# Inverse sequence products in five blocks of 128 frequencies instead of six, with a shifted sine table

## The chip, the cores and the metric

The kernel runs on one core of a Trainium2 chip. The time is device microseconds of one execution, as the median of several runs. The profile shows one further execution in detail: TensorE (PE, with its weight loads as PEld), VectorE (DVE), ScalarE (ACT), GpSimd (POOL), SyncE's DMA queue (SP), and the DMA engines.

## The reference

A spectral layer and a gated feed-forward layer, both on one sequence of S = 2048 rows and D = 576 columns, in bf16:

```python
x = A_x                                         # (1, 2048, 576)
X = rfft2(layernorm(x))                         # 2048 x 289 complex
y = irfft2(X * (w_r + 1j * w_i), s=(2048, 576)) # to bf16
h = x + y
n = layernorm(h)
out = h + (gelu(n @ w_gate) * (n @ w_up)) @ w_down   # 576 -> 4608 -> 576, tanh gelu
```

## The kernel before

Both transforms are matrix products. Row s of the sequence is written as 16·p + h, with p on the 128 partitions and h = 0..15 in the free dimension, so that the transform over 2048 rows splits into one over 16 and one over 128. The column transform over 576 uses only J = 289 frequencies (JP = 290 with one column of padding, JH = 145 of each parity).

The spectral layer has these stages on TensorE.

- `row16` (L259, L268): normalised rows times the table of the 16-point transform, with some filler products (L247). ScalarE copies the results to `Bt`.
- A loop over nine sequence frequencies in the order k = 1, 2, ..., 7, 0 (`order`; k = 0 also carries k = 8). One round of the loop takes care of three different groups at once: `f2` (L442) is the column transform of the newest group, `f3` (L457, L458) the 128-point transform of the group before, and `i3` (L541, L542) the first inverse product of the group three rounds back. ScalarE copies each result from PSUM to SBUF (`pq`, `g`, `hs`, `EO`).
- Between `f3` and `i3`, VectorE forms sums (`sums_of`, L487 and L488), multiplies with the complex weights `WR`, `WI` (L505), combines the four products (L511, L512), and writes the result to one of three buffers `Zt` (L516, L517). The group k = 0 is done in two halves of the columns, 0 to 127 and 128 to 288, and L511 and L512 write `Zt` directly.
- `inv_cols` (L568): the inverse column product, for half `x` of the groups and a pair `g` of rows h. ScalarE evicts the result.
- `add_rows` (L680): the inverse 16-point product. VectorE adds it to `h_sb`.

`Zt` holds four rows of JP = 290 columns: cosine and sine parts b = 0, 1, and the same with the roles exchanged (a = 1). The inverse product `i3` has the columns as output partitions. It takes them in NJT = 3 tiles of 128, the last with 33 columns and zeros behind them (each buffer has 96 columns of zeros at its end), for both b: 3 x 2 blocks, each of two matmuls (a = 0, 1) of 256 columns. So a group has 12 matmuls, and `EO` has six blocks:

```python
EO = [eop.tile([P, 2, NJT, H, 2, 4, 8], ...) for x in range(2)]
lhsT=EO[x][:, e, jt, 2 * g : 2 * g + 2], rhs=DT[:, jt, :, e, :] if jt < 2 else DI[:, :, e, :]
```

`DT` holds the cosine (e = 0) and sine (e = 1) tables of the columns 0 to 255, `DI` those of the last 33, `D3` is what `DI` is copied from in `late_tables` (L396). ScalarE computes `DT` and `D3` at L310 and L311. `TF` and `TI` are the twiddle tables; `TI` is the transposition of `TF` by a DMA on SP in `twiddles` (L382), followed on that queue by the load of `wd_a`.

The head of the feed-forward layer comes next. `add_sum` adds the inverse result to rows h = 0 to 3, and the sums for the second layernorm come with it (VectorE for the sum, ScalarE for the squares). `head_rstd` makes the mean and `rstd2` from them: two small operations on VectorE (L734, L737) and two on GpSimd (L738, and the power at L739). `norm2` and `flip` normalise rows 0 and 1 and transpose them by DMA (L717); `norm_row` and `turn` do it for rows 2 and 3 with transpositions on TensorE (L747), whose result is copied to `hl[0]` in two parts, by ScalarE (L750) and VectorE (L751). Products of `inv_cols` stand between these steps and keep TensorE busy. PSUM is used through a rotation of four double banks with the tag `two`.

Then come four blocks of 512 rows of the feed-forward layer: 36 gate/up products each (L815), with gelu on ScalarE (L823) and the product on VectorE (L824), and the down products (L835). The remaining rows are normalised beside the first of these.

The order on every engine is the order of the program text (a manual schedule); waits follow from the data.

Of the kernel before, what the change touches and what calls it, by code (L numbers as in the profile page):

```python
# [20 lines left out]
P = 128  # L21
# [9 lines left out]
NR = D // 64  # L31
NDT = 5
NJT = 3
FQ = 3
PI = 3.1415925
G_SCALE = 2.0 ** -10
# [4 lines left out]
def kernel_body(  # L41
# [65 lines left out]
    DT = keep.tile([P, 2, 2, 2, JH], BF16, name="DT")  # L107
    DF = keep.tile([P, 2, 2, JH], BF16, name="DF")
    DI = keep.tile([P, 2, 2, JH], BF16, name="DI")
    mv = keep.tile([P, H, 2], FP32, name="mv")  # L110
    rstd = keep.tile([P, H], FP32, name="rstd")
    mv2 = keep.tile([P, H, 2], FP32, name="mv2")
# [50 lines left out]

    TF = sp.tile([P, 9, 3, P], BF16, name="TF")
    TI = sp.tile([P, 9, 3, P], BF16, name="TI")
    Zts = [sp.tile([P, 4 * JP + 96], BF16, name=f"Zt{i}") for i in range(3)]

    scr_pool = tc.tile_pool(name="scr", bufs=1, side="right")
    scr = scr_pool.__enter__()
# [160 lines left out]
    V.tensor_scalar(F16[:, 2, :], F16[:, 0, :], -1.0, None, op0=ALU.mult)  # L330
    ln_rstd(rstd, mv, 0, 4)
    for z in Zts:
        G.memset(z[:, 4 * JP :], 0.0)
        G.memset(z[:, J : 4 * JP : JP], 0.0)
    sd(4, 6)
    fin(5, 7)
    norms(0, 4)
# [40 lines left out]


    def twiddles():  # L380
        A.activation(TF[:, :, 1, :], ab[:], ACT.Sin, bias=nhpib[:], scale=2.0 * PI / S)
        nc.sync.dma_start(  # L382
            TI[:].rearrange("p k r q -> p (k r) q"), TF[:].rearrange("p k r q -> p (k r q)"), transpose=True
        )
        nc.sync.dma_start(wd_a[:], wd_view[:, 0:NWA, :])

    def weights():

# [4 lines left out]
            V.tensor_scalar(w[:, :, 0 : J : J - 1], w[:, :, 0 : J : J - 1], 0.5, None, op0=ALU.mult)  # L393

    def late_tables():
        V.tensor_copy(DI[0 : J - 2 * P], D3[0 : J - 2 * P])  # L396
        pt = two("pt")
        for x in range(2):
            for p0 in (0, 64):
                T.matmul(  # L400
                    pt[p0 : p0 + 64, 0, x * P : (x + 1) * P],
                    lhsT=F16[:, 0, 64 * x : 64 * x + 64],
                    rhs=ident[:],
                    start=True,
                    stop=True,
                )
# [83 lines left out]
    def wmul(k, i, nxt=None):  # L490
        x = xab[k]
        z = Zts[i % 3]
        zt[k] = z
        zv = z[:, 0 : 4 * JP].rearrange("p (a b j) -> p a b j", a=2, b=2)
        sl = slice(k, 18 - k, 17 - 2 * k) if k else slice(0, 9, 8)
        m1, m2 = (wk.tile([P, 2, 2, JP], BF16, name=n, tag=n, bufs=1) for n in ("m1", "m2"))
        if k:
            za, zb = (wk.tile([P, 2, JP], BF16, name=n, tag=n, bufs=1) for n in ("za", "zb"))
        else:
            za, zb = zv[:, 0], zv[:, 1]  # L500

        for j0, j1 in ((0, J),) if k else ((0, P), (P, J)):
            js = slice(j0, j1)
            for w, m in ((WR, m1), (WI, m2)):
                V.tensor_tensor(  # L505
                    m[:, :, :, js],
                    x[:, :, :, js],
                    w[:, sl, js].unsqueeze(1).to_broadcast([P, 2, 2, j1 - j0]),
                    ALU.mult,
                )  # L510
            V.tensor_tensor(za[:, :, js], m1[:, 0, :, js], m2[:, 1, :, js], ALU.subtract)  # L511
            V.tensor_tensor(zb[:, :, js], m1[:, 1, :, js], m2[:, 0, :, js], ALU.add)  # L512
            if nxt:
                sums_of(nxt)
            if k:
                V.tensor_tensor(zv[:, 0, :, js], za[:, :, js], zb[:, ::-1, js], ALU.add)  # L516
                V.tensor_tensor(zv[:, 1, :, js], zb[:, ::-1, js], za[:, :, js], ALU.subtract)  # L517

    eo = {}

    def i3(k, jt):


        z = zt[k]
        x, i = place[k]

        def zl(a, b):
            o = (2 * a + b) * JP + jt * P
            return z[:, o : o + P]

        n = 2 if k and jt < 2 else 1
        if jt == 0 or n == 1:
            eo[k] = two("eo_ps")
        if k:
            ps = eo[k][:].rearrange("p b (n h e l) -> p b n e h l", n=2, h=H, l=8)[:, :, jt % n]
            parts = ((0, k, (0, 0), (1, 1)), (1, k, (0, 1), (1, 0)))
        else:
            ps = eo[k][:, 0, :].rearrange("p (e h b l) -> p b e h l", e=2, h=H, l=8)
            parts = ((0, 0, (0, 0), (1, 0)), (1, 8, (0, 1), (1, 1)))
        for b, kk_, z0, z1 in parts:  # L540
            T.matmul(ps[:, b], lhsT=zl(*z0), rhs=TI[:, kk_, 1:3, :], start=True, stop=False)  # L541
            T.matmul(ps[:, b], lhsT=zl(*z1), rhs=TI[:, kk_, 0:2, :], start=False, stop=True)  # L542
        if n == 2:
            if jt == 1:
                A.copy(
                    EO[x][:, :, 0:2, :, :, i, :].rearrange("p b t h e l -> p b (t h e) l"),
                    eo[k][:].rearrange("p b (r l) -> p b r l", l=8),
                )
        elif k:
            A.copy(  # L550
                EO[x][:, :, jt, :, :, i, :].rearrange("p b h e l -> p b (h e) l"),
                eo[k][:, :, 0 : 2 * P].rearrange("p b (r l) -> p b r l", l=8),
            )
        else:
            (V.tensor_copy if jt == 1 else A.copy)(
                EO[x][:, :, jt, :, :, i, :].rearrange("p e h b l -> p e (h b) l"),
                eo[k][:, 0, :].rearrange("p (e r l) -> p e r l", e=2, l=8),
            )

    cs = {}  # L560
# [2 lines left out]
    def inv_cols(x, g):  # L563

        ps = two("cs_ps")
        for e in range(2):
            for jt in range(NJT):
                T.matmul(  # L568
                    ps[:, e, 0:JP],
                    lhsT=EO[x][:, e, jt, 2 * g : 2 * g + 2].rearrange("p h e k l -> p (h e k l)"),  # L570
                    rhs=DT[:, jt, :, e, :] if jt < 2 else DI[:, :, e, :],
                    start=(jt == 0),
                    stop=(jt == NJT - 1),
                )
# [22 lines left out]
    for i in range(n + 1):  # L597
# [26 lines left out]
        if i == 1:  # L624
            late_tables()
            scr_pool.__exit__(None, None, None)
            eop = ctx.enter_context(tc.tile_pool(name="eop", bufs=1, side="right"))
            EO = [eop.tile([P, 2, NJT, H, 2, 4, 8], BF16, name=f"EO{x}", tag=f"EO{x}") for x in range(2)]
    for g in range(3):
        inv_cols(0, g)  # L630
    for k in order[6:]:
# [99 lines left out]
    def head_rstd(h):  # L731


        V.scalar_tensor_tensor(  # L734
            mv2[:, h, 1:2], sums[:, h, 0:1], sums[:, h, 0:1], sums[:, h, 1:2], op0=ALU.mult, op1=ALU.subtract
        )
        V.tensor_scalar(mv2[:, h, 0:1], sums[:, h, 0:1], 1.0 / D, None, op0=ALU.mult)  # L737
        G.tensor_scalar(rstd2[:, h : h + 1], mv2[:, h, 1:2], -1.0 / (D * D), 1e-5, op0=ALU.mult, op1=ALU.add)  # L738
        G.tensor_tensor(rstd2[:, h : h + 1], rstd2[:, h : h + 1], mhalf[:, h : h + 1], ALU.pow)  # L739

    def turn(h):


        pt = psum.tile([P, 2048], BF16, name="pt", tag="two", bufs=4)
        for r in range(NR):
            for p0 in (0, 64):
                T.transpose(pt[p0 : p0 + 64, r * P : (r + 1) * P], ln2[h][:, r * 64 : (r + 1) * 64], ident[:])  # L747
        q = h % 4 * P
        pv = pt[:, 0 : NR * P].rearrange("p (r q) -> p r q", r=NR)
# [32 lines left out]
    turn(2)  # L782
    turn(3)
    inv_cols(1, 6)
    inv_cols(1, 7)
    load_wd(2)

# [113 lines left out]
```

## Time and profile before

| | |
|---|---|
| median of 3 runs | 509.99 us (509.99 to 509.99) |
| profiled execution | 509.67 us, its span 507.4 us |
| granted clock of TensorE in it | 1.0 |
| PE busy | 496.0 us (98%) |
| DVE, ACT, POOL busy | 213.9, 154.5, 33.1 us |
| L815 (gate/up) on the chain that ended last | 55% |
| L835 (down) on it | 28% |
| first gate/up matmul | 78.74 us after the start of the span |

The chain that ended last lies on TensorE for 94% of the span. All that the change edits lies ahead of the first gate/up matmul, that is, in the first 79 of 507 us. In the lines of a timeline the columns are: start, duration, engine, line, operation, output and inputs, shape, count; the idle time ahead of it and what ended that idle time stand in brackets. A matmul's duration includes its passage through the array; what one costs in a dense stream is the distance between two starts (its pitch).

### The profile page before, as it was taken

How to read it: one execution, taken by the hardware profiler on the slowest of the kernel's cores; microseconds unless marked ns; L12 is line 12 of the kernel's file. 1: busy time of each engine (PE TensorE's matmuls, PEld its weight loads, DVE VectorE, ACT ScalarE, POOL GpSimd, SP SyncE). 2: the span in 40 equal slices, each digit the busy share in tenths (PEclk: the TensorE clock that was granted, in tenths of full speed). 3: DMA queues.
4: the chain of work that ended last, by engine and by line, in shares of the span. 5: the costliest groups of instructions: out<-in, count | busy, mean ns of one | idle time of the engine just before them, and what ended most of it. 6: DMA issues, size and time to landing. Idle time of an engine off the chain costs nothing.

```text
span 507.4 us, 9925 instructions
## 1 busy us (share of the span) xinstructions
PE 496.0 (98%) x4357; PEld 288.9 (57%) x4357; DVE 213.9 (42%) x414; ACT 154.5 (30%) x266; POOL 33.1 (7%) x88
## 2 busy tenths in 40 slices
PE   6989999999999999999999999999999999999997
PEld 2557775444447774444467744444577544444775
DVE  8979963689661015433311034433201233333001
ACT  8688985322230002323310023233200132323000
POOL 8700020111110000000000000000000000000000
PEclk9999999999999999999999999999999999999999
DMA  8964057779970019997720089987500578770000
GB/s 290 237 139 141 1 165 206 148 149 195 191 143 1 0 43 199 180 201 151 149 63 0 1 186 198 182 166 152 101 1 0 119 163 158 157 152 2 13 12 25
DMA packets 86090, 60.66 MB, mean 120 GB/s; under 512 B 21920, under 2 KB 84768, under 8 KB 86048
## 3 DMA queue, kind: packets, MB, share of 16 engines
q1 hardware_dynamic: 85760, 58.85, 57.3%
q0 software_dynamic: 288, 1.18, 0.8%
q8 instruction: 34, 0.56, 0.5%
q14 instruction: 8, 0.07, 0.1%
HBM read 52.65 MB, written 2.36 MB: 108 GB/s over the span
## 4 chain that ended last, share of the span: by engine, by line
PE 94%; DVE 3%; ACT 1%; issue 0%; POOL 0%; POOLq 0%; ACTq 0%; DVEq 0%
PE gu L815 55%; PE acc L835 28%; PE cs_ps L568 2%; PE f2t L259 1%; PE pq_ps L442 1%; PE y_ps L680 1%; PE eo_ps L542 1%; PE eo_ps L541 1%; PE f2t L247 1%; PE gh_ps L457 1%; PE gh_ps L458 1%; PE f L268 1%; DVE st L119 0%; DVE st L118 0%; DVE m L505 0%
## 5 line engine op out<-in xcount | busy, mean ns | idle before, releaser
L815 PE MATMUL gu<-Bt,wgu 64*128 64x512 bf16 x2592 | 281.4, 376 | 0.0
L815 PEld LDWEIGHTS <-wgu 64*128 64x128 bf16 x2592 | 126.1, 94 | 152.2 <-issue 1.0
L823 ACT ACTIVATE g_sb<-gu 128x512 f32<-128x512 f32 x144 | 86.0, 597 | 301.9 <-PE gu L815 301.8
L824 DVE TENSOR_TENSOR P_sb<-g_sb,gu 128x512 bf16<-128x512 f32 x144 | 98.7, 685 | 151.7 <-ACT g_sb L823 151.7
L835 PEld LDWEIGHTS <-P_sb 128*128 128x128 bf16 x1152 | 112.4, 98 | 30.6 <-issue 2.4
L835 PE MATMUL acc<-wd,P_sb 128*128 128x288 bf16 x768 | 99.3, 286 | 0.0
L847 DVE TENSOR_TENSOR h_sb<-h_sb,acc 128x576 bf16<-128x576 bf16 x15 | 11.3, 754 | 118.2 <-PE acc L835 118.2
L835 PE MATMUL acc<-wd_a,P_sb 128*128 128x288 bf16 x384 | 52.3, 286 | 0.5 <-DVE h_sb L843 0.5
L247 PE MATMUL f2t<-h_sb,ident 128*128 128x512 bf16 x41 | 13.6, 459 | 4.4 <-DMA h_sb<-in_A_x_dram 4.4
L442 PE MATMUL pq_ps<-DT,Bt 128*128 128x290 bf16 x64 | 12.4, 286 | 0.0
L705 DVE TENSOR_SCALAR hrow<-h_sb,mv,rstd 128x1152 bf16<-128x1152 bf16 x14 | 12.1, 867 | 0.5 <-POOL rstd L739 0.5
L568 PE MATMUL cs_ps<-DT,EO 128*128 128x290 bf16 x64 | 12.2, 286 | 0.0
L247 PEld LDWEIGHTS <-ident 128*128 128x128 bf16 x45 | 5.0, 111 | 12.3 <-issue 6.6
L541 PE MATMUL eo_ps<-TI,Zt 128*128 128x256 bf16 x48 | 11.5, 272 | 0.4 <-DVE Zt L516 0.4
L542 PE MATMUL eo_ps<-TI,Zt 128*128 128x256 bf16 x48 | 11.5, 273 | 0.1
L136 POOL TENSOR_TENSOR rstd<-rstd,mhalf 128x1 f32<-128x1 f32 (+2 forms) x17 | 11.4, 673 | 1.4
L135 POOL TENSOR_SCALAR rstd<-mv 128x1 f32<-128x1 f32 (+2 forms) x17 | 4.0, 238 | 108.9 <-DVE mv L120 108.7
L568 PEld LDWEIGHTS <-EO 128*128 128x128 bf16 x96 | 9.0, 96 | 3.0 <-issue 0.2
L442 PEld LDWEIGHTS <-Bt 128*128 128x128 bf16 x96 | 9.2, 97 | 2.5
L450 ACT CAST pq<-pq_ps 128x580 bf16<-128x580 f32 x15 | 9.9, 660 | 0.9 <-PE pq_ps L442 0.8
L259 PE MATMUL f2t<-F,xn 128*128 128x256 bf16 x64 | 9.7, 273 | 0.3 <-DVE xn L139 0.3
L118 DVE BATCH_NORM_STATS2 st<-h_sb 128x6 f32<-128x288 bf16 x22 | 9.8, 445 | 0.0
(132 smaller groups left out, 261.0 us busy)
## 6 DMA issues: line engine op xcount, KB each, us to landing
wgu<-in_B_w_gate_dram SPq DMA_DIRECT2D x48, 432.0 KB, 5.1
wgu<-in_B_w_up_dram SPq DMA_DIRECT2D x48, 432.0 KB, 6.6
wd<-in_B_w_down_dram SPq DMA_DIRECT2D x2, 1728.0 KB, 8.0
h_sb<-in_A_x_dram SPq DMA_DIRECT2D x3, 576.0 KB, 5.9
wd_a<-in_B_w_down_dram SPq DMA_DIRECT2D x1, 1728.0 KB, 9.4
out_dram<-h_sb SPq DMA_DIRECT2D x3, 576.0 KB, 3.3
WR<-in_A_w_r_dram SPq DMA_DIRECT2D x1, 650.2 KB, 8.7
WI<-in_A_w_i_dram SPq DMA_DIRECT2D x1, 650.2 KB, 11.0
```

The costliest lines, as they stand in the source:

```text
L136: G.tensor_tensor(dst[:, sl], dst[:, sl], mhalf[:, sl], ALU.pow)
L247: T.matmul(dst, lhsT=ident[:], rhs=h_sb[:, 2, 0:512], start=True, stop=True)
L259: T.matmul(f2t[:, h % 2, t * 2 * P : (t + 1) * 2 * P], lhsT=x[:, d0 : d0 + P], rhs=F16[:, n : n + 2, :], start=(n == 0), stop=(n == 1),)
L442: T.matmul(ps[:, par, 0:JP], lhsT=Bt[:, t, col], rhs=DT[:, t // 2, par] if t < 4 else DF[:, par], start=(t == par), stop=(t == 4),)
L541: T.matmul(ps[:, b], lhsT=zl(*z0), rhs=TI[:, kk_, 1:3, :], start=True, stop=False)
L542: T.matmul(ps[:, b], lhsT=zl(*z1), rhs=TI[:, kk_, 0:2, :], start=False, stop=True)
L568: T.matmul(ps[:, e, 0:JP], lhsT=EO[x][:, e, jt, 2 * g : 2 * g + 2].rearrange("p h e k l -> p (h e k l)"), rhs=DT[:, jt, :, e, :] if jt < 2 ...
L705: V.tensor_scalar(hrow[:], h_sb[:, h, :].rearrange("p (r k) -> p r k", k=64).unsqueeze(2).to_broadcast([P, NR, 2, 64]), mv2[:, h, 0:1], rs ...
L815: T.matmul(gu[:, c, :], lhsT=w[rows, r, i * P : (i + 1) * P], rhs=hl[tcnk % 2][rows, r, :], start=(r == 0), stop=(r == NR - 1),)
L823: A.activation(g_sb[:], gu[:, 0, :], ACT.Gelu_apprx_tanh)
L824: V.tensor_tensor(p_sb(fa + i), g_sb[:], gu[:, 1, :], ALU.mult)
L835: T.matmul(acc[:, c, 0:DH], lhsT=p_sb(f)[:, st * P : (st + 1) * P], rhs=wd[f // NWA][:, f % NWA, cc], start=(f == 0), stop=(f == NFT - 1),)
```

## The change

`Zt` becomes four rows of ZS = 320 columns, 289 used and 31 zeros. For k = 1 to 7 the rows of the two parts b lie one behind the other, 640 columns, and the inverse product takes them in five tiles of 128: tiles 0 and 1 are columns 0 to 255 of b = 0, tile 2 holds columns 256 to 319 of b = 0 and 0 to 63 of b = 1, tiles 3 and 4 are columns 64 to 319 of b = 1. That makes ten matmuls of 256 columns per group. L517's operands change so that the parts lie in the order that this needs.

For the sine part, the column product now needs a table that begins at column 64. This is the new `DS`; it and the second half of the sine part of `DI` are filled by five copies by DMA on the SP queue, ahead of the transposition of the twiddles. `DI`'s copy on VectorE takes only the cosine part.

For k = 0 (and 8) the two parts come from different twiddles. There the five tiles are formed from 24 matmuls of 128 columns in place of 12 of 256; the last eight have 64 output partitions each, four for the lower and four for the upper half.

ScalarE's `EO` copies per group k = 1 to 7 are one of four blocks and one of one block (before: four and two).

In the head, the scaling for `rstd2` moves from GpSimd to VectorE, `head_rstd(3)` moves ahead of `norm2(1)`, `turn` uses one PSUM tile with one VectorE copy for row 2 and two tiles with a ScalarE and a VectorE copy for row 3, and `inv_cols(1, 6)` moves ahead of both `turn` calls. The memsets of `Zt` on GpSimd become three instead of six.

The order of TensorE's other products, of VectorE's frequency loop and of all of the feed-forward layer stays.

```diff
+ZS = 320
+    DS = keep.tile([P, 2, 2, JH], BF16, name="DS")
-    Zts = [sp.tile([P, 4 * JP + 96], BF16, name=f"Zt{i}") for i in range(3)]
+    Zts = [sp.tile([P, 4, ZS], BF16, name=f"Zt{i}") for i in range(3)]
...
     for z in Zts:
-        G.memset(z[:, 4 * JP :], 0.0)
-        G.memset(z[:, J : 4 * JP : JP], 0.0)
+        G.memset(z[:, :, J:], 0.0)
...
     def twiddles():
+        sine_rows()
...
+    def sine_rows():
+        for dst, src in (
+            (DI[64:128, :, 1, :], DT[0:64, 0, :, 1, :]),
+            (DS[0:64, 0, :, :], DT[64:128, 0, :, 1, :]),
+            (DS[64:128, 0, :, :], DT[0:64, 1, :, 1, :]),
+            (DS[0:64, 1, :, :], DT[64:128, 1, :, 1, :]),
+            (DS[64:128, 1, :, :], D3[0:64, :, 1, :]),
+        ):
+            nc.sync.dma_start(dst, src)
...
     def late_tables():
-        V.tensor_copy(DI[0 : J - 2 * P], D3[0 : J - 2 * P])
+        V.tensor_copy(DI[0 : J - 2 * P, :, 0, :], D3[0 : J - 2 * P, :, 0, :])
...
-                V.tensor_tensor(zv[:, 1, :, js], zb[:, ::-1, js], za[:, :, js], ALU.subtract)
+                V.tensor_tensor(zv[:, 1, :, js], zb[:, :, js], za[:, ::-1, js], ALU.subtract)
...
-    def i3(k, jt):
+    def i3(k, s):
...
+            for n, w in (((0, 0), (1, 1)), ((2, 3), (3, 4)), ((0, 2),))[s]:
+                o = w * P
+                T.matmul(pv[:, n], lhsT=z[:, o : o + P], rhs=TI[:, k, 1:3, :], start=True, stop=False)
+                o += 2 * ZS
+                T.matmul(pv[:, n], lhsT=z[:, o : o + P], rhs=TI[:, k, 0:2, :], start=False, stop=True)
...
+        for n, c, j, p0, m in (
+            ((0, 0, 0, 0, P), (1, 0, P, 0, P)),
+            ((2, 1, 64, 0, P), (3, 1, 192, 0, P)),
+            ((0, 0, 256, 0, 64), (0, 1, 0, 64, 64)),
+        )[s]:
+            for b in range(2):
+                for a in range(2):
+                    T.matmul(
+                        pv[p0 : p0 + m, n, b],
+                        lhsT=z[:, (2 * a + b) * ZS + j : (2 * a + b) * ZS + j + m],
+                        rhs=TI[:, 8 * b, 1 - a + c, :],
+                        start=(a == 0),
+                        stop=(a == 1),
+                    )
...
-                    lhsT=EO[x][:, e, jt, 2 * g : 2 * g + 2].rearrange("p h e k l -> p (h e k l)"),
-                    rhs=DT[:, jt, :, e, :] if jt < 2 else DI[:, :, e, :],
+                    lhsT=EO[x][:, 2 * e + jt if jt < 2 else 4, 2 * g : 2 * g + 2].rearrange("p h e k l -> p (h e k l)"),
+                    rhs=DI[:, :, e, :] if jt == 2 else DS[:, jt] if e else DT[:, jt, :, 0, :],
...
+        V.tensor_scalar(rstd2[:, h : h + 1], mv2[:, h, 1:2], -1.0 / (D * D), 1e-5, op0=ALU.mult, op1=ALU.add)
         V.tensor_scalar(mv2[:, h, 0:1], sums[:, h, 0:1], 1.0 / D, None, op0=ALU.mult)
-        G.tensor_scalar(rstd2[:, h : h + 1], mv2[:, h, 1:2], -1.0 / (D * D), 1e-5, op0=ALU.mult, op1=ALU.add)
...
-        pt = psum.tile([P, 2048], BF16, name="pt", tag="two", bufs=4)
...
-        A.copy(hl[0][:, 0:5, q : q + P], pv[:, 0:5])
-        V.tensor_copy(hl[0][:, 5:NR, q : q + P], pv[:, 5:NR])
+        parts = ((V.tensor_copy, 0, NR),) if h == 2 else ((A.copy, 0, 4), (V.tensor_copy, 4, NR))
+        for copy, r0, r1 in parts:
+            pt = psum.tile([P, 2048], BF16, name="pt", tag="two", bufs=4)
...
+    head_rstd(3)
     norm2(1)
     flip(1)
-    head_rstd(3)
...
-    for g in range(3, 6):
+    for g in range(3, 7):
         inv_cols(1, g)
     turn(2)
     turn(3)
-    inv_cols(1, 6)
     inv_cols(1, 7)
```

More of the change, by code (lines that the diff above doesn't have):

```diff
@@ L493, in wmul @@
         zt[k] = z
-        zv = z[:, 0 : 4 * JP].rearrange("p (a b j) -> p a b j", a=2, b=2)
+        zv = z[:].rearrange("p (a b) j -> p a b j", a=2)
         sl = slice(k, 18 - k, 17 - 2 * k) if k else slice(0, 9, 8)
@@ L516, in wmul @@
                 V.tensor_tensor(zv[:, 0, :, js], za[:, :, js], zb[:, ::-1, js], ALU.add)
-                V.tensor_tensor(zv[:, 1, :, js], zb[:, ::-1, js], za[:, :, js], ALU.subtract)
+                V.tensor_tensor(zv[:, 1, :, js], zb[:, :, js], za[:, ::-1, js], ALU.subtract)
     eo = {}
-    def i3(k, jt):
-        z = zt[k]
+    def i3(k, s):
         x, i = place[k]
[L527 to L532, printed above, removed]
+        z = zt[k][:].rearrange("p c j -> p (c j)")
+        if s != 1:
@@ L533, in i3 @@
             eo[k] = two("eo_ps")
+        ps = eo[k]
         if k:
[L535 to L542, printed above, removed]
@@ L543, in i3 @@
-        if n == 2:
-            if jt == 1:
+            pv = ps[:].rearrange("p a (n h e l) -> p (a n) e h l", n=2, h=H, l=8)
+            for n, w in (((0, 0), (1, 1)), ((2, 3), (3, 4)), ((0, 2),))[s]:
[3 more added lines that the diff above has]
+                T.matmul(pv[:, n], lhsT=z[:, o : o + P], rhs=TI[:, k, 0:2, :], start=False, stop=True)
+            if s == 1:
                 A.copy(
-                    EO[x][:, :, 0:2, :, :, i, :].rearrange("p b t h e l -> p b (t h e) l"),
-                    eo[k][:].rearrange("p b (r l) -> p b r l", l=8),
-                )
[L549 to L552, printed above, removed]
-            )
-        else:
-            (V.tensor_copy if jt == 1 else A.copy)(
-                EO[x][:, :, jt, :, :, i, :].rearrange("p e h b l -> p e (h b) l"),
-                eo[k][:, 0, :].rearrange("p (e r l) -> p e r l", e=2, l=8),
+                    EO[x][:, 0:4, :, :, i, :].rearrange("p w h e l -> p w (h e) l"),
+                    ps[:].rearrange("p a (n r l) -> p (a n) r l", n=2, l=8),
+                )
+            elif s == 2:
+                A.copy(
+                    EO[x][:, 4, :, :, i, :].rearrange("p h e l -> p (h e) l"),
+                    ps[:, 0, 0 : 2 * P].rearrange("p (r l) -> p r l", l=8),
+                )
@@ new lines, in i3 @@
+            return
+        pv = ps[:].rearrange("p a (n h b l) -> p (a n) b h l", n=2, h=H, l=8)
+        for n, c, j, p0, m in (
[11 more added lines that the diff above has]
+                        stop=(a == 1),
+                    )
@@ L558, in i3 @@
+        if s < 2:
+            (V.tensor_copy if s else A.copy)(
+                EO[x][:, 2 * s : 2 * s + 2, :, :, i, :].rearrange("p w h e l -> p w (h e) l"),
+                ps[:, s].rearrange("p (n r l) -> p n r l", n=2, l=8),
+            )
+        else:
+            A.copy(
+                EO[x][:, 4, :, :, i, :].rearrange("p h e l -> p (h e) l"),
+                ps[:, 0, 0 : 2 * P].rearrange("p (r l) -> p r l", l=8),
             )
@@ L627, in kernel_body @@
             eop = ctx.enter_context(tc.tile_pool(name="eop", bufs=1, side="right"))
-            EO = [eop.tile([P, 2, NJT, H, 2, 4, 8], BF16, name=f"EO{x}", tag=f"EO{x}") for x in range(2)]
+            EO = [eop.tile([P, 5, H, 2, 4, 8], BF16, name=f"EO{x}", tag=f"EO{x}") for x in range(2)]
     for g in range(3):
@@ L736, in head_rstd @@
         )
+        V.tensor_scalar(rstd2[:, h : h + 1], mv2[:, h, 1:2], -1.0 / (D * D), 1e-5, op0=ALU.mult, op1=ALU.add)
         V.tensor_scalar(mv2[:, h, 0:1], sums[:, h, 0:1], 1.0 / D, None, op0=ALU.mult)
-        G.tensor_scalar(rstd2[:, h : h + 1], mv2[:, h, 1:2], -1.0 / (D * D), 1e-5, op0=ALU.mult, op1=ALU.add)
         G.tensor_tensor(rstd2[:, h : h + 1], rstd2[:, h : h + 1], mhalf[:, h : h + 1], ALU.pow)
     def turn(h):
-        pt = psum.tile([P, 2048], BF16, name="pt", tag="two", bufs=4)
-        for r in range(NR):
-            for p0 in (0, 64):
-                T.transpose(pt[p0 : p0 + 64, r * P : (r + 1) * P], ln2[h][:, r * 64 : (r + 1) * 64], ident[:])
         q = h % 4 * P
-        pv = pt[:, 0 : NR * P].rearrange("p (r q) -> p r q", r=NR)
-        A.copy(hl[0][:, 0:5, q : q + P], pv[:, 0:5])
-        V.tensor_copy(hl[0][:, 5:NR, q : q + P], pv[:, 5:NR])
+        parts = ((V.tensor_copy, 0, NR),) if h == 2 else ((A.copy, 0, 4), (V.tensor_copy, 4, NR))
+        for copy, r0, r1 in parts:
+            pt = psum.tile([P, 2048], BF16, name="pt", tag="two", bufs=4)
+            for r in range(r0, r1):
+                for p0 in (0, 64):
+                    T.transpose(pt[p0 : p0 + 64, r * P : (r + 1) * P], ln2[h][:, r * 64 : (r + 1) * 64], ident[:])
+            copy(
+                hl[0][:, r0:r1, q : q + P],
+                pt[:, r0 * P : r1 * P].rearrange("p (r q) -> p r q", q=P),
+            )
     def norm_row(h):
```

## Prediction

> **What bounds the kernel now.** I read the page first: the engines' shares and the groups that the change edits.
>
> ```profile
> PE 496.0 (98%) x4357; PEld 288.9 (57%) x4357; DVE 213.9 (42%) x414; ACT 154.5 (30%) x266; POOL 33.1 (7%) x88
> ...
> L541 PE MATMUL eo_ps<-TI,Zt 128*128 128x256 bf16 x48 | 11.5, 272 | 0.4 <-DVE Zt L516 0.4
> L542 PE MATMUL eo_ps<-TI,Zt 128*128 128x256 bf16 x48 | 11.5, 273 | 0.1
> ```
>
> TensorE fills 98% of the span, and its only recorded idle time in the two inverse lines is 0.4 us, behind VectorE's `Zt`. But 98% is an average. The edited work lies between 36 and 79 us, so next comes that stretch, engine by engine. The timeline of TensorE gives the pitch of the frequency loop (first inverse matmul of the groups k=2, 3 and 4) and its last stretch:
>
> ```profile
> 43.63 0.27 PE L541 MATMUL eo_ps<-TI,Zt 128*128 128x256 bf16 x1
> ...
> 47.41 0.27 PE L541 MATMUL eo_ps<-TI,Zt 128*128 128x256 bf16 x1
> ...
> 51.19 0.27 PE L541 MATMUL eo_ps<-TI,Zt 128*128 128x256 bf16 x1
> ...
> 64.31 0.28 PE L542 MATMUL eo_ps<-TI,Zt 128*128 128x256 bf16 x1
> ...
> 65.30 0.41 PE L568 MATMUL cs_ps<-DT,EO 128*128 128x290 bf16 x2
> ```
>
> TensorE's period is 47.41 - 43.63 = 3.78 us, with no gap: 12 matmuls of L541/L542 at a pitch of 0.109 (1.31), 12 of L442 (1.48) and 8 of L457/L458 (0.99) make 3.78. The timeline of VectorE over the same loop, with its end:
>
> ```profile
> 39.81 0.76 DVE L505 TENSOR_TENSOR m<-xab,WR 128x1156 bf16<-128x1156 bf16 x1
> ...
> 43.51 0.76 DVE L505 TENSOR_TENSOR m<-xab,WR 128x1156 bf16<-128x1156 bf16 x1
> ...
> 47.21 0.76 DVE L505 TENSOR_TENSOR m<-xab,WR 128x1156 bf16<-128x1156 bf16 x1
> ...
> 63.93 0.33 DVE L512 TENSOR_TENSOR Zt<-m,m 128x322 bf16<-128x322 bf16 x1
> ```
>
> VectorE's period is 3.70 us, also with no idle time shown from 36 to 60 us. So TensorE leads it by only 0.08 us of load per group. `Zt` of k=2 is finished at 43.51 and read at 43.63; of k=3 at 47.21 and 47.41. VectorE's last operation of the whole chain (second half of k=0) ends at 63.93 + 0.33 = 64.26, and TensorE's matmul at 64.31 starts right behind it. Nine matmuls (9 x 0.109 = 0.98) follow up to 65.30. From there to the first gate/up matmul at 78.74 TensorE has no gap but about 0.1 us at each change of tile shape.
>
> **Products of k=1 to 7: ten matmuls each, not twelve.** Saved: 14 x 0.109 = 1.53 us of TensorE. Its period would be 3.78 - 0.22 = 3.56, under VectorE's 3.70, whose eight operations per group keep their sizes (only the reversed operand of L517 moves to the other input). VectorE's start does not move either: its first `xab` (35.15) waits for ScalarE, which waits for the twiddle table, all upstream of the change. So TensorE now waits some 0.14 us per group for `Zt`, and the 1.53 becomes waiting. Group k=7 cannot start before L517 of k=7 ends (61.48, wait and queue about 61.6), ends at about 62.7 (it was 63.9), and then the second half of k=0 is still missing until 64.26. ScalarE's second copy per group halves from 512 elements; ScalarE is off this path, so nothing.
>
> **`late_tables`.** The DI copy shrinks from 33x580 in one run to two runs of 145 per partition. It sits in VectorE's chain at 35.9 and takes 0.21 there. Bounds: half the work is gone (-0.07, keeping some 0.06 of fixed cost), or a slower rate of one element per ns, about 0.36 (+0.15). The copy L390 with rows of 289 runs at 2312/0.67 = 3.4 elements per ns, also short odd rows, so I take -0.07: the chain ends at 64.19, the first matmul that needs it starts at 64.24.
>
> **k=0: 24 matmuls of 128 columns in place of 12 of 256.** Of the new list, those of the first block pair's first half (four) and one more need only what VectorE has written by 64.0. Nineteen come behind 64.24: three of step 0, eight of step 1, eight of step 2, the last with 64 output partitions. At a pitch p, and 0.1 us each for going to the 64-wide shape and back, the products end at 64.24 + 19p + 0.2, against 65.30: a shift of 19p - 0.86. No row has a full 128x128 weight with 128 columns. From below, p is half of 0.109, 0.0545 (the columns alone): +0.18. From above it is 0.109, as a shorter stream should not be slower than the longer one: +1.21. The nearest row with 128 columns per matmul is the transposition of the head, which also prices the change of shape:
>
> ```profile
> 75.80 0.28 PE L568 MATMUL cs_ps<-DI,EO 128*128 128x290 bf16 x1
> 76.01 1.20 PE L747 MATMUL pt<-ident,hflat 128*64 128x128 bf16 x36
> 77.14 0.42 PE L568 MATMUL cs_ps<-DT,EO 128*128 128x290 bf16 x2
> ```
>
> L568 has a pitch of 0.124, so 75.80 should be followed at 75.92, and 76.01 is 0.09 late: the change of shape. The 36 then take 1.13, or 0.063 for each pair on the two halves of the array. The weight loads of L747 last 110 ns each, far over 63, so a load's recorded length is no floor for the pitch; those of 128x128 last 97. I take p = 0.063: 19 x 0.063 - 0.86 = **+0.34**. For the shape change the Trainium skill (TensorEngine Tiling (Array Packing), Key Properties) says that changing the tiling mode drains the engine; the 0.09 here agrees.
>
> **Five copies of the sine table, ahead of the twiddle transposition on SP.** The DMA queue's waits:
>
> ```profile
> SPq L382 <- DVE TF L377: 10.1, 1, 10.1
> ```
>
> SP's last weight load is issued by 21.06 and the transposition goes out at 33.20, so SP idles there 10 us. Five issues of 0.4 to 0.6 us (as for `wd_a`, 0.58) fit; their sources, the sine rows of `DT` and `D3`, are written by ScalarE by 12.8. Their data stand behind the weights, which have landed by about 30. Nothing, and without that cover 2.5 us on the transposition, whose landing (33.20 + 5.2 = 38.4) is needed at 39.58. wd_a moves alike.
>
> **Pads of Zt.** GpSimd does three memsets of 4x31 for six of 96 and 4 elements (13.03 to 13.52); its next `rstd` is ready at 16.69 and used at 17.24. Nothing, either way up to 0.5.
>
> **Head.** TensorE is dense from 65.30 to 78.74, so an earlier `rstd2` buys nothing; what counts is that nothing gets late. `norm2(1)` moves behind `head_rstd(3)`, some 0.3 later on VectorE, but the two `flip` transpositions go out back to back (2.76 us from 73.43), so SP sets the second; it lands at 74.81 + 3.3 = 78.1, used at 78.74. `turn` is the same 36 transpositions, now behind `inv_cols(1, 6)`: only one product (0.745) stands between them and gate/up. VectorE's copy for head 2 grows to 1152 elements: at L751's 0.42 for 512 up to 0.95, from about 77.5 to 78.5, against 78.74. Cost 0, with 0.2 left; beyond that it is paid in full. Bounds 0 to +0.2.
>
> **Sum.** The profiled execution has a span of 507.4 and a time of 509.67, so 2.27 lie around the span; the median of the runs is 509.99, 0.32 above it. Profile: 509.67 + 0.34 = 510.0; median: **510.3**.
>
> **Rivals.** *Weight loads set the pitch (slower).* Place: the nineteen short matmuls behind 64.24. If a weight is not loaded under a stream of 128 columns, p is near 97 ns, and for the eight 64-wide ones, which now follow each other on the same half where L747 alternates halves, up to 0.11 + 0.055. Then 11 x 0.097 + 8 x 0.165 + 0.2 + 64.24 - 65.30 = +1.53: 511.5. It passes 0.2% (1.02 us, about what a measurement of this kernel can tell from no change) from a mean p of 0.099. For it: no row shows such a pitch. Against it: 110 ns loads in L747 at 63 ns. The Trainium skill (TensorE: Matmul & The Clock Gate, Back-to-back issue gap) gives about 81 ns per matmul of 128 columns in a stream with weight loads; no run so far shows it, and by that figure 19p - 0.86 would be an estimated +0.68.
>
> *VectorE is not the bound (faster).* Then all 1.53 counts against k=0's extra 24 x 0.063 + 0.2 - 1.31 = 0.40: -1.13, 509.9 - 1.1 = 508.9. It needs a VectorE period under 3.56 or a chain that starts earlier; the rows show neither.
>
> *A new wait in the head (slower).* If VectorE's copy for head 2, or the flips, come 1 us late, gate/up waits by as much: 511.3. The margins of 0.2 and 0.6 speak against it.
>
> *The change does nothing.* If TensorE's waits for `Zt` stretch less and k=0's short products overlap, the shift is -0.1 to +0.1: 510.0.
>
> **Numbers.** Forecast (p from 0.0545 to 0.099): 0.56. Weight loads: 0.22. Late head or late tables: 0.10. Nothing: 0.06. Faster: 0.06. So faster 0.06, same 0.62, slower 0.32. The range goes from 509.7 (forecast at its low end, the DI copy and a little of the faster case) to 511.6 (weight loads at 511.5); outside are most of the faster case and a head later than 1.3 us.
>
> **What would show it.** In the profile after: VectorE's period still 3.70 and its last L526 ending at 64.2; TensorE with some 0.1 us idle per group and about 0.9 before the second half of k=0, all released by `Zt`; the k=0 products ending at 65.6; gate/up starting at 79.1. I am wrong on size if the pitch of the k=0 products is not near 0.063, and wrong on mechanism if gate/up starts before 78.7 or if the last `Zt` ends before 63.9.

## The result, and the profile after

The changed kernel takes 510.64 us in the median (20 runs, 510.32 to 512.08) against 509.99 (20 runs): a ratio of 1.0016, interval 1.0009 to 1.0023. It is 0.65 us slower; 510.3 was forecast. The profiled execution took 510.62 us with a span of 508.4.

Two things help to compare runs this close. Most runs of a kernel fall on levels about 0.3 us apart that are set ahead of the changed work, and the profiled executions of three experiments (e1, e5 and e11 below) had a granted clock of 0.997 and started VectorE's chain 1.2 us later or more (36.66, 37.03 and 36.66), so I count positions from the start of that chain (its first `xab`): 35.15 in the kernel before, 35.42 in the changed one. And time less span is constant within a kernel to about 0.1 us, but between kernels it goes from 1.8 to 2.3 us; differences under 0.5 us are read from the spans.

The page's line of the engines, then TensorE's timeline: the first inverse matmul of the groups k = 2, 3 and 4, two rows of `f3` between, and the last stretch.

```profile
PE 494.4 (97%) x4353; PEld 287.0 (56%) x4355; DVE 214.7 (42%) x418; ACT 152.4 (30%) x265; POOL 32.6 (6%) x81
```

```profile
43.75 0.27 PE L547 MATMUL eo_ps<-TI,Zt 128*128 128x256 bf16 x1
...
47.46 0.27 PE L547 MATMUL eo_ps<-TI,Zt 128*128 128x256 bf16 x1
...
50.53 0.28 PE L471 MATMUL gh_ps<-pq,TF 128*128 128x289 bf16 x1
50.80 0.28 PE L472 MATMUL gh_ps<-pq,TF 128*128 128x289 bf16 x1
...
51.16 0.27 PE L547 MATMUL eo_ps<-TI,Zt 128*128 128x256 bf16 x1
...
63.37 0.39 PE L570 MATMUL eo_ps<-TI,Zt 128*128 128x128 bf16 x4
64.25 0.58 PE L570 MATMUL eo_ps<-TI,Zt 128*128 128x128 bf16 x4 [0.50 <-DVE Zt L525]
65.50 0.96 PE L570 MATMUL eo_ps<-TI,Zt 128*128 128x128 bf16 x16 [0.67 <-ACT EO L578]
66.39 0.42 PE L596 MATMUL cs_ps<-DT,EO 128*128 128x290 bf16 x2
```

TensorE is busy for 1.6 us less, and the kernel is slower. The period is 47.46 - 43.75 = 3.71, not TensorE's own 3.56: the saved products have become waiting. Where the waiting lies is not where I put it, though. The products of the inverse line come at their 0.109; L472 stands 0.27 behind L471 in place of 0.125. And among the products of k = 0 a second wait has appeared, behind ScalarE (`EO`, L578). The timelines of VectorE (its period, and the chain's end) and of ScalarE (one round, and the end) say what TensorE waits for:

```profile
43.70 0.76 DVE L519 TENSOR_TENSOR m<-xab,WR 128x1156 bf16<-128x1156 bf16 x1
...
47.40 0.76 DVE L519 TENSOR_TENSOR m<-xab,WR 128x1156 bf16<-128x1156 bf16 x1
...
64.11 0.33 DVE L526 TENSOR_TENSOR Zt<-m,m 128x322 bf16<-128x322 bf16 x1
```

```profile
48.64 0.64 ACT L492 CAST hs<-gh_ps 128x578 bf16<-128x578 f32 x1 [0.23 <-PE gh_ps L472]
49.18 1.02 ACT L551 CAST EO<-eo_ps 128x1024 bf16<-128x1024 f32 x1
50.08 0.66 ACT L464 CAST pq<-pq_ps 128x580 bf16<-128x580 f32 x1
...
52.35 0.64 ACT L492 CAST hs<-gh_ps 128x578 bf16<-128x578 f32 x1 [0.23 <-PE gh_ps L472]
...
64.86 0.58 ACT L578 CAST EO<-eo_ps 128x512 bf16<-128x512 f32 x1 [0.23 <-PE eo_ps L570]
```

VectorE's period is still 3.70, and its chain ends at 64.44. But ScalarE's copy of `pq` ends at 50.08 + 0.66 = 50.74, and L472 starts at 50.80, right behind it. That copy stands behind the `EO` copy, that one behind `hs`, and `hs` waits for the products that L472 opens: a loop through both engines with a period of 52.35 - 48.64 = 3.71. Two bounds lie side by side: over four rounds VectorE takes 14.80 and this loop 14.82.

In the kernel before, the same loop was already close. ScalarE's copy of `pq` ended there at 50.04 + 0.66 = 50.70, only 0.12 ahead of the product L458 that reads it, and with no wait in between. ScalarE's timeline before, then TensorE's:

```profile
50.04 0.66 ACT L450 CAST pq<-pq_ps 128x580 bf16<-128x580 f32 x1
```

```profile
50.70 0.28 PE L457 MATMUL gh_ps<-pq,TF 128*128 128x289 bf16 x1
50.82 0.29 PE L458 MATMUL gh_ps<-pq,TF 128*128 128x289 bf16 x1
```

At the end, ScalarE copies step 0 of k = 0 from 64.86 to 65.44, and step 1 starts at 65.50. Step 1 writes the other bank of the same PSUM tile (`eo[k]` is only renewed where `s != 1`), so the program makes it wait for the copy. In the kernel before, each step of k = 0 had a tile of its own.

Gate/up starts at 79.82, that is 44.40 behind the start of VectorE's chain; before it was 78.74 - 35.15 = 43.59. The 0.81 between them, less 0.1 made up later, is the 0.7 by which the shortest spans differ.

### The profile page after: what moved, and what is told of

Read it like the earlier page. It is cut to its first block, busy times and chain, and to the rows that moved or that the text cites. A ratio compares the mean times of both kernels' runs of the same rounds, so it can differ in the third digit from the quotient of the medians.

```text
span 508.4 us, 9921 instructions
## 1 busy us (share of the span) xinstructions
PE 494.4 (97%) x4353; PEld 287.0 (56%) x4355; DVE 214.7 (42%) x418; ACT 152.4 (30%) x265; POOL 32.6 (6%) x81
## 4 chain that ended last, share of the span: by engine, by line
PE 90%; DVE 7%; ACT 1%; DMA 1%; issue 0%; POOL 0%; DVEq 0%; ACTq 0%
PE gu L845 55%; PE acc L865 28%; DVE m L519 2%; PE cs_ps L596 2%; PE f2t L261 2%; PE y_ps L708 1%; DVE za L525 1%; DMA h_sb<-in_A_x_dram 1%; PE f2t L249 1%; DVE xab L502 1%; PE f L270 1%; DVE Zt L530 1%; DVE zb L526 1%; DVE Zt L531 1%; DVE xab L501 0%
## 5 line engine op out<-in xcount | busy, mean ns | idle before, releaser
L249 PE MATMUL f2t<-h_sb,ident 128*128 128x512 bf16 x39 | 11.9, 434 | 4.4 <-DMA h_sb<-in_A_x_dram 4.4
L120 DVE BATCH_NORM_STATS2 st<-h_sb 128x6 f32<-128x288 bf16 x22 | 9.8, 444 | 0.0
L121 DVE BATCH_NORM_STATS2 st<-h_sb 128x6 f32<-128x288 bf16 x22 | 9.7, 442 | 0.0
L471 PE MATMUL gh_ps<-pq,TF 128*128 128x289 bf16 x32 | 8.6, 286 | 1.1 <-ACT pq L464 0.6
L280 ACT CAST Bt<-f2t 128x1024 bf16<-128x1024 f32 x8 | 8.1, 1011 | 4.4 <-PE f2t L261 4.4
```

The source lines that it names most:

```text
L249: T.matmul(dst, lhsT=ident[:], rhs=h_sb[:, 2, 0:512], start=True, stop=True)
```

## The experiments

This table has every run. "G" is the start of gate/up behind the start of VectorE's chain, "period" that of TensorE's rounds, "span" the shortest span of the runs. A difference of 0.01 in the period is within rounding.

| kernel | median us | ratio to before, interval | span | period | G |
|---|---|---|---|---|---|
| before | 509.99 | | 507.4 | 3.78 | 43.59 |
| changed | 510.64 | 1.0016 (1.0009 to 1.0023) | 508.1 | 3.71 | 44.40 |
| e1 own PSUM tile | 509.42 | 0.9991 (0.9982 to 0.9999) | 507.2 | 3.71 | 43.57 |
| e2 old head | 510.30 | 1.0003 (0.9993 to 1.0012) | 508.1 | 3.70 | 44.39 |
| e3 e1, products ahead of k = 0 | 509.01 | 0.9981 (0.9973 to 0.9990) | 506.8 | 3.71 | 43.13 |
| e4 e1, a sum on GpSimd | 513.99 | 1.0070 (1.0057 to 1.0083) | 511.6 | 4.41 | 47.88 |
| e5 before, no `zb` | 509.35 | 0.9992 (0.9983 to 1.0001) | 507.0 | 3.78 | 43.23 |
| e6 e1, no `zb` | 508.82 | 0.9972 (0.9959 to 0.9986) | 506.4 | 3.70 | 42.69 |
| e7 e3, early sine | 508.79 | 0.9974 (0.9964 to 0.9984) | 506.3 | 3.70 | 43.37 |
| e8 before, new head | 509.50 | 0.9990 (0.9980 to 1.0000) | 507.5 | 3.78 | 43.56 |
| e9 e1, `pq` copy first | 509.94 | 1.0003 (0.9993 to 1.0012) | 507.8 | 3.91 | 44.17 |
| e10 e9, no `zb` | 509.56 | 0.9996 (0.9986 to 1.0005) | 507.3 | 3.91 | 43.59 |
| e11 e1, split copy | 509.06 | 0.9980 (0.9971 to 0.9990) | 507.2 | 3.70 | 43.58 |
| e12 e11, no `zb` | 507.94 | 0.9953 (0.9935 to 0.9972) | 505.8 | 3.56 | 42.14 |

**e1: an own PSUM tile for step 1 of k = 0.**

```diff
-        if s != 1:
+        if s != 1 or not k:
             eo[k] = two("eo_ps")
```

> The changed kernel with one more PSUM tile: step 1 of group k=0 gets its own, where it shared one with step 0. Theory W (a wait that the change brought in: step 1's first matmul waits until ScalarE has copied step 0 out of the shared tile): in the changed kernel step 1 would have started at 64.66 and started at 65.50, so 0.84 us go; TensorE goes from step 0 to step 1 without a gap, time 510.65 - 0.84 = 509.8. Rival P (the short matmuls of k=0 themselves are slow, and what stands behind them would be late anyway): the time stays within 0.2 of 510.6.

G falls by 0.83, to that of the kernel before, and the span by 0.9. TensorE's timeline has no gap left behind VectorE's last write (20 products in 66.80 - 65.49):

```profile
65.49 1.38 PE L570 MATMUL eo_ps<-TI,Zt 128*128 128x128 bf16 x20 [0.49 <-DVE Zt L525]
66.80 0.42 PE L596 MATMUL cs_ps<-DT,EO 128*128 128x290 bf16 x2
```

So the wait for the shared tile is the slowdown: without it the rest of the change is worth nothing measurable up to gate/up. The median fell by 1.22: 0.9 in the span, 0.1 around it, and the rest because the two medians lie on different levels.

**e2: the changed kernel with the old head; e8: the kernel before with the new head.** The edit is the head's part of the diff, undone or done alone (in e2 all other parts stay, in e8 none is there).

> The changed kernel with the head of the kernel before (scaling for rstd2 on GpSimd, order of head_rstd, turn and inv_cols as before). Theory: TensorE has no gap from the k=0 products to gate/up in either, so the head's part of the change is worth nothing: within 0.15 of 510.65. Rival H (the new head is what costs, for instance VectorE's longer copy ahead of gate/up): 510.0 or less.

> The kernel before with nothing of the change but the reordered head (rstd on VectorE, the split turns, the products of one column group moved). Inside the span nothing is expected (the gate and up products start as far behind VectorE's chain start as in the kernel before, 43.6 us): 510.0. If the 0.3 us that the version with the old head differed from the changed kernel around its span comes with the new head, 510.3.

Both times missed what I expected. The two edits are opposite, and yet each makes its kernel faster: the old head in the changed kernel saves 0.34, the new head in the old kernel saves 0.49. Inside the span neither does anything: G is 44.39 against 44.40, and 43.56 against 43.59. The difference is in the time less span, which is 2.2 for the changed kernel, 1.9 for e2, 2.3 for the kernel before and 1.8 for e8. As the new head goes with more in one pair and less in the other, the head alone does not account for it. What sets it stays open.

**e3: e1, with three products of the first column pairs drawn ahead of k = 0**, so that TensorE has work while VectorE finishes k = 0.

```diff
     for k in order[6:]:
+        if k == 0:
+            inv_cols(0, 3)
         for jt in range(NJT):
             i3(k, jt)
-    inv_cols(0, 3)
+    inv_cols(0, 4)
```

(The later calls of `inv_cols(0, g)` each move up by one place.)

> e1 with one column product (x=0, g=3; 0.745 us) moved ahead of group k=0, and those that fill the head each one place earlier. Theory V (VectorE's chain, not TensorE's work, sets when the second half of k=0 starts): the product fills the gap of about 0.65 us in which TensorE waits for the last Zt, so some 0.6 us are gained on e1: 509.2; up to 0.3 of it may be lost again where gate/up then waits for the DMA transpositions of rows 0 and 1, so 509.2 to 509.5. Rival (TensorE's own work sets it): a mere exchange of order, the same as e1.

The mechanism came as expected: the 24 products of k = 0 run without a gap, G falls by 0.44 against e1, and the second transposed row of the head becomes the next wait, 0.24 at gate/up. The time lies below the expected 509.2 to 509.5 because e1 itself came out 0.4 faster than I had expected. TensorE's timeline, k = 0 and what follows, then gate/up:

```profile
63.80 1.50 PE L570 MATMUL eo_ps<-TI,Zt 128*128 128x128 bf16 x24
65.24 0.42 PE L596 MATMUL cs_ps<-DT,EO 128*128 128x290 bf16 x2
...
78.24 6.00 PE L846 MATMUL gu<-Bt,wgu 64*128 64x512 bf16 x54 [0.24 <-DMA Bt<-hrow]
```

**e4: e1, with the sum of L501 on GpSimd from the second group on**, to make VectorE's period 3.33.

```diff
-    def sums_of(k):
+    def sums_of(k, E=V):
...
-        V.tensor_tensor(x[:, 0, :, 0:J], g[:, :, 0:J], hs[:, :, 0:J], ALU.subtract)
+        E.tensor_tensor(x[:, 0, :, 0:J], g[:, :, 0:J], hs[:, :, 0:J], ALU.subtract)
...
-                sums_of(nxt)
+                sums_of(nxt, G)
```

> e1 with one of the two sums per group (L501 of the changed kernel, 0.37 us of VectorE) on GpSimd from the second group on. Theory V: VectorE's period falls from 3.70 to about 3.33 and TensorE's saved products show: its period becomes 3.56 and the time 508.7 (e1 less 1.1), if GpSimd takes under 1.9 us for the sum and does not slow VectorE. If VectorE is not the bound: the same as e1. If GpSimd is slower or slows VectorE: the same or slower than e1, with VectorE's other operations longer in the trace.

VectorE got slower, not faster: its own sum, alone at 0.46, takes 1.55 beside GpSimd's. The timelines of VectorE and of GpSimd at the same moment:

```profile
42.96 1.55 DVE L502 TENSOR_TENSOR xab<-g,hs 128x578 bf16<-128x578 bf16 x1
```

```profile
42.70 1.49 POOL L501 TENSOR_TENSOR xab<-g,hs 128x578 bf16<-128x578 bf16 x1 [2.92 <-ACT hs L492]
```

VectorE's period became 4.41, TensorE's followed, and the time rose by 4.6 against e1, 4.2 of it six rounds of 0.7. That shows that a slower VectorE sets the pace, not yet that it alone does.

**e5 and e6: `zb` left out**, which does make VectorE quicker: its own work falls to 3.33 a round. Part of the computation is missing then (`za` stands in for `zb`), so these kernels, and e10 and e12, only serve to find the bounds.

```diff
-            za, zb = (wk.tile([P, 2, JP], BF16, name=n, tag=n, bufs=1) for n in ("za", "zb"))
+            za = zb = wk.tile([P, 2, JP], BF16, name="za", tag="za", bufs=1)
...
-            V.tensor_tensor(zb[:, :, js], m1[:, 1, :, js], m2[:, 0, :, js], ALU.add)
+            if not k:
+                V.tensor_tensor(zb[:, :, js], m1[:, 1, :, js], m2[:, 0, :, js], ALU.add)
```

> The kernel before, with the sum zb left out for the groups k=1 to 7 (za is used in its place, so that part of the computation is missing). It takes 0.37 us of VectorE out of each group: VectorE's period falls from 3.70 to about 3.33, below TensorE's 3.78. If TensorE's own products set the pitch of the groups in the kernel before once VectorE is quick enough (theory: VectorE and TensorE stood nearly level there), the time falls by the little that TensorE still waited plus the shorter lead-out of the last group: 509.6, with groups still about 3.78 apart in TensorE. If VectorE alone set the pitch, groups come 3.33 apart and the time is about 507.4.

> The changed kernel with an own PSUM tile for step 1 of k=0, and with the sum zb left out for the groups k=1 to 7 in the same way. If VectorE was what hid the saved products of the groups, TensorE's period now falls to the 3.56 of its own work, and the time is about 1.2 below that of the same kernel with zb: 508.2, and about 1.4 below the kernel before without zb (14 saved products of 0.109 us less 0.1). If the saved products did not shorten TensorE's work in the groups at all (the rival that weight loads or something else set the pitch), the period stays near 3.70 and the time at 509.4.

The period of e5 came out as expected, and its time 0.25 below: in the kernel before, TensorE's own products set 3.78. e6 did not: 3.56 was expected and the period stayed at 3.70. VectorE now idles, and TensorE still waits at L472. VectorE's timeline of e6, then TensorE's:

```profile
49.11 0.47 DVE L501 TENSOR_TENSOR xab<-g,hs 128x578 bf16<-128x578 bf16 x1 [0.28 <-ACT hs L492]
```

```profile
50.31 0.28 PE L471 MATMUL gh_ps<-pq,TF 128*128 128x289 bf16 x1
50.59 0.28 PE L472 MATMUL gh_ps<-pq,TF 128*128 128x289 bf16 x1
```

The 0.88 that e6 gains in G comes from the end of the chain, where VectorE's last groups no longer trail. My theory that VectorE alone covers the saved products fell here; the loop through ScalarE took its place.

**e7: e3, with the second sine activation of the twiddle table ahead of the first group's copies on ScalarE.**

```diff
     def twiddles():
         sine_rows()
-        A.activation(TF[:, :, 1, :], ab[:], ACT.Sin, bias=nhpib[:], scale=2.0 * PI / S)
...
+    A.activation(TF[:, :, 1, :], ab[:], ACT.Sin, bias=nhpib[:], scale=2.0 * PI / S)
     n = len(order)
     for i in range(n + 1):
```

> The kernel with the own PSUM tile and the cosine-table products drawn ahead of k=0, and now the second sine activation of the twiddle table issued on ScalarE before the copies of the first group, where TensorE's first f3 products waited 0.46 us for it. If the start of VectorE's chain sets the time of everything behind it, the chain starts about 0.45 earlier and the time is about 508.55. Rival: the copies of the first group are pushed back by as much as the activation comes forward, or a later transfer is awaited in its place, and the time stays at 509.0.

About half of it: 0.22 in the median. The two profiled executions lie on different levels, e3's on its lowest (span 506.8, chain start 35.11) and e7's on a higher one (506.9, where its shortest is 506.3; chain start 34.93). Kernels without this edit start the chain at 35.41 to 35.45 on the higher level, so it seems to have come forward by about 0.5, as expected; of that 0.24 is lost again, because the head's second transposed row makes gate/up wait 0.48 in place of 0.24. The shortest spans differ by 0.5, but only one run of e7 is that short. This is the fastest of the kernels that leave nothing out.

**e9 and e10: the copy of `pq` ahead of the `EO` copy on ScalarE**, without and with `zb` left out, to break the loop.

```diff
             if s == 1:
-                A.copy(
+                late.append((
                     EO[x][:, 0:4, :, :, i, :].rearrange("p w h e l -> p w (h e) l"),
                     ps[:].rearrange("p a (n r l) -> p (a n) r l", n=2, l=8),
-                )
+                ))
...
             f2(order[i] + 8)
+            if late:
+                A.copy(*late.pop())
```

> The changed kernel with the own PSUM tile for step 1 of k=0, and on ScalarE the copy of pq (580 elements) now issued ahead of the EO copy of 1024 elements in each group. Theory, new after the last runs: since the change TensorE's groups are held by two bounds at once, VectorE's 3.70 and a loop of 3.71 through ScalarE, whose copy of pq stands behind the EO copy (0.90) while TensorE waits about 0.15 a group for it. Breaking that loop alone leaves VectorE's 3.70: period 3.70, time 509.4 like the kernel without the swap, and TensorE's 0.15 a group now behind VectorE or ScalarE at another place. If ScalarE's loop was the only bound, the period is 3.56 and the time about 508.4.

> The same with the sum zb left out for k=1 to 7 (za in its place, that part of the computation is missing), so that both bounds are lifted: VectorE could do 3.33 and the pq copy is ahead of the EO copy. Theory: only now the ten products a group show, TensorE's period is its own 3.56 and the time 0.7 to 0.9 below that of the kernel without zb alone (six groups of 0.15), 508.0. Rivals: another loop through ScalarE or a PSUM tile that is free later (the EO copy now ends 0.5 later) holds the period at 3.7 or more, and the time is 508.8 or above.

Neither period is the expected one; the second rival of e10, a PSUM tile that is free later, came true in both. L472 no longer waits, but the `EO` copy now ends later and holds its PSUM tile; TensorE's first inverse product waits for that, and the period is 3.91 (51.51 - 47.60) with `zb` and without. TensorE's timeline of e9:

```profile
47.60 0.27 PE L551 MATMUL eo_ps<-TI,Zt 128*128 128x256 bf16 x1 [0.19 <-ACT EO L652]
...
51.51 0.27 PE L551 MATMUL eo_ps<-TI,Zt 128*128 128x256 bf16 x1 [0.19 <-ACT EO L652]
```

**e11 and e12: the `EO` copy in two halves**, one ahead of `pq` and one behind it, so that the loop gets shorter and the tile is free in time.

```diff
             if s == 1:
-                A.copy(EO[x][:, 0:4, ...], ps[:]...)
+                for a in range(2):
+                    late.append((EO[x][:, 2 * a : 2 * a + 2, ...], ps[:, a]...))
+                    if a == 0 or k in (6, 7):
+                        A.copy(*late.pop())
...
             f2(order[i] + 8)
+            if late:
+                A.copy(*late.pop())
```

> The changed kernel with the own PSUM tile for step 1 of k=0, and the EO copy of 1024 elements in each group split in two of 512: one stays ahead of the copy of pq on ScalarE, the other goes behind it. This takes about 0.4 us out of the loop through ScalarE (3.71) without holding the PSUM tile as long as when the whole copy went behind (there the period was 3.91, set by a product waiting for that tile). VectorE alone is left as a bound above TensorE's 3.56: period 3.70, time 509.4 like the kernel without the split. If VectorE is no bound of its own and only followed the loop, 3.56 and about 508.5.

> The same with the sum zb left out for k=1 to 7 (za in its place, that part of the computation is missing). Both bounds are lifted: TensorE's period 3.56, no wait at the second product of a group, and 0.7 to 0.9 below the kernel without zb alone (508.8): 508.0. If a further loop through ScalarE or PSUM holds it, the period is 3.6 to 3.7 and the time 508.3 to 508.8.

Both periods are as expected. In e11 the loop is broken and the period stays at VectorE's 3.70; the gap now stands behind the engine that the prediction had named, at the second inverse product, which waits for VectorE's last write of `Zt` (L531, 48.27 + 0.46 = 48.73). In e12 both bounds are lifted, there is no gap, and the period is TensorE's own 3.56. TensorE's timeline of e11, then of e12:

```profile
48.55 0.27 PE L548 MATMUL eo_ps<-TI,Zt 128*128 128x256 bf16 x1
48.79 0.28 PE L550 MATMUL eo_ps<-TI,Zt 128*128 128x256 bf16 x1
```

```profile
46.95 0.27 PE L549 MATMUL eo_ps<-TI,Zt 128*128 128x256 bf16 x1
...
50.52 0.27 PE L549 MATMUL eo_ps<-TI,Zt 128*128 128x256 bf16 x1
```

e1, e6, e11 and e12 are the four corners: lift VectorE's bound alone and the period is 3.70, lift ScalarE's alone and it is 3.70, lift both and it is 3.56. With `zb` out of both, five blocks beat six by 1.2 us of span (e12 against e5; e12 also has the own tile and the split copy). No kernel that leaves nothing out has a period under 3.70. (The median of e11 is 0.36 below that of e1 at equal spans; that again lies around the span.)

## Why the prediction was right or wrong

- **Direction and size.** Forecast +0.3 on the median, measured +0.65. That the measured time lies near the forecast is partly luck: two errors of opposite sign stand behind it, products of k = 0 priced 0.33 too high and a wait of 0.83 left out.
- **The 1.53 us of saved products become waiting.** Right. By the end of the chain nothing of it is left: with an own tile, G is 43.57 against 43.59.
- **"So TensorE now waits some 0.14 us per group for `Zt`".** The amount is right (0.145 at L472), the releaser is wrong. The step that failed is the sentence that ScalarE "is off this path, so nothing": its loop has a period of 3.71 (14.82 in four rounds, against VectorE's 14.80). I had looked at VectorE's period alone. ScalarE was nearly full in the kernel before, too: its timeline there has 0.09 us of idle time in a round of 3.78.
- **`late_tables` -0.07.** Right: the copy's place in VectorE's chain shrank from 0.21 to 0.14 us, and the chain ends 29.02 after its start, before 64.26 - 35.15 = 29.11.
- **k = 0: 19p + 0.2 at p = 0.063.** Too dear. In e1 VectorE's last write ends at 65.68; from 65.73 to 66.80 are 1.07 us, so 19p + 0.2 = 1.07 and p = 0.046, below the lower bound of 0.0545. The eight products of step 1 do run at 0.055 (0.44 for eight); the eight with 64 output partitions are cheaper, since two halves of the array overlap although they are issued four and four. In the changed kernel they and the changes of shape take 66.39 - 65.50 - 0.44 = 0.45. My bound missed that; it made the forecast 0.33 too high.
- **The wait for the shared PSUM tile.** Not in the sum, nor among the rivals: 0.83 (e1). The condition `if s != 1` is in the code, and I read it as a matter of k = 1 to 7, where no copy lies between the two steps. The sum then is 0.34 - 0.33 - 0.02 + 0.83 = 0.82, against 0.81 in G.
- **The rival of weight loads.** Its condition, a mean pitch from 0.099, did not come: the 128x128 loads last 97 ns in the list of groups and hide at 0.055 per product. The Trainium skill (TensorE: Matmul & The Clock Gate, Back-to-back issue gap) gives about 81 ns per matmul of 128 columns; this stream, with its own weights for each product, went at 55, so the measurement decides.
- **The rival that VectorE is not the bound (-1.13).** The saving it priced exists, but only with both bounds lifted.
- **Copies of the sine table at nothing.** Right, with less left than I said. The first of the five issues took 2.30 us where I allowed 0.4 to 0.6, and all five lasted from 23.14 to 28.08. SP's timeline shows the last copy issued 5.4 us ahead of the transposition:

```profile
27.49 0.59 SPq L399 DMA_DIRECT2D DS<-D  x1
33.47 4.22 SPq L384 DMA_TRANSPOSE TI<-TF  x1
```

  The transposition of the twiddles took 6.1 us from issue to landing in every kernel with the copies, and 5.0 to 5.2 in the three without (before, e5, e8). It landed at 33.47 + 6.1 = 39.6 where `Zt` lets the product start at 39.78. Without `zb`, it is the wait itself (e12: 0.27). Whether the copies cause the 0.9 was not tried.
- **Head and pads at nothing.** Right inside the span (e2, e8); nothing waits for the pads' memsets.
- **What would show it.** VectorE's 3.70 and the end of its chain came as said (64.44 less the 0.27 by which the chain starts later); the products of k = 0 ended 0.5 later than my 65.6 on the same clock, and gate/up 0.45 later than 79.1. That all waits are released by `Zt` did not come: L472 and step 1 of k = 0 wait for ScalarE.

## What to carry to other kernels

When a change takes work off the busiest engine, write down the period of every engine and of every loop through two engines in that stage, not only the one that is next: here two bounds lay within 0.01 us of each other (14.80 and 14.82 in four rounds), and neither could be seen behind the other until one was lifted. When a change regroups products, check which PSUM tile each one writes and what copies from that tile in between; a second tile cost nothing that the runs show here and was worth 0.83 us. Small differences are read from the span, and from a fixed point in it, before an edit is credited with them.

## What the runs showed of the hardware

- A sum on VectorE beside one on GpSimd took 1.55 us in place of 0.46, and ended some 0.3 behind GpSimd's, which took 1.34 to 1.49 (e4). What GpSimd's sum takes alone, no run shows. The Trainium skill (GPSIMD Engine Reference, Specifications) says that GpSimd shares its SBUF interfaces with VectorE and contends with instructions that have two SBUF inputs; the trace agrees for this sum, which has two. The sum just ahead of it on VectorE (L526) has two as well and stayed at 0.46, though its last 0.2 to 0.35 us lie within GpSimd's recorded time; the recorded ends of GpSimd's instructions are rough. The loss is larger than what was moved.
- Products with 64 output partitions on two halves of the array overlap even when four of one half are issued before four of the other. One by one, the trace of the changed kernel has them start in pairs, at 66.04 and 66.05, 66.12 and 66.13, 66.17 and 66.19, 66.23 and 66.24. Going to this shape and back costs 0.09 each, as in the row of L747. The list of groups of the changed kernel between 62 and 68 us has them beside the full ones (busy us, mean ns of one, idle time before them):

```profile
L570 PE MATMUL eo_ps<-TI,Zt 128*128 128x128 bf16 x16 | 1.6, 220 | 1.2 <-ACT EO L578 0.7 <-DVE Zt L525 0.5
L570 PE MATMUL eo_ps<-TI,Zt 128*64 128x128 bf16 x8 | 0.4, 225 | 0.0
```

- Time less span differs by up to 0.5 us between kernels whose spans are equal to 0.1 us (1.8 in e8, 2.3 before), and by about 0.1 between runs of one kernel. What sets it was not found.
